# A gated mix of two long convolutions: a twisted length-2048 transform, a smaller set of kernel positions and no turn through DRAM

## The chip, the cores and the metric

The kernel runs on one core of a Trainium2 chip. The metric is the device time of one execution in microseconds (us). The engines are called PE (matrix multiply; its weight loads are shown apart as PEld), DVE (vector), ACT (scalar), POOL and SP; the last two mostly issue transfers here.

## The reference

Two branches act on 2048 positions of 448 channels, and a gate mixes them.

```
g = sigmoid((u * gate_w).sum(channels))                  # one number for each position
dt = exp(log_dt);  l = bf16(0 .. 2047)                   # positions rounded to bf16
K[d, l] = real(sum over 256 modes n of C[d,n] * exp(dt[d]*A[d,n]*l) * dt[d]*B[d,n])
a = causal_convolution(K, u) + u * Dskip                 # by a padded FFT of 4096
kv = (sum over t of 4 of k[l - t] * shift_k[d, t]) * v
b = u * (causal_convolution(ssm_k, kv) + kv * ssm_D)
out = g * a + (1 - g) * b
```

Because the positions are rounded to bf16, only 641 different values of l occur among the 2048: all up to 256, then every second, every fourth and every eighth.

## The kernel before

A position is split as 64a + b with a below 32 and b below 64, and a channel as a group g (4), a part h (2) and an index dd (56). The transform works on matrices of 128 rows.

**Setup** (`Weights`, `kgen_load`, `kgen_setup`, L23 to L411) builds the cosine matrices and the table of powers of the modes. Power level k+1 is the square of level k in float32, eleven levels by four DVE operations each (L408 to L411); each is written in bf16 to a DRAM scratch `ed` and read back block by block as `kg_E`.

**The SSM kernel K** is made by `KGen.block` in 14 blocks of 32 channels (64 modes to a partition). DVE multiplies up all powers by `cmul` (L427 to L434: one product over four planes into `kg_P`, one sum), a table `TQ` of 32 entries and a table `TP` of 8 by 8; ACT spreads factors (`kg_Ex`, L481). Then 128 matmuls of 32 weight columns and 64 moving columns give the block's K at all 2048 positions (L516), and ACT copies it into `xcK`.

**The convolutions** run in four halves (branch B halves 0 and 1, then branch A halves 0 and 1), each by `conv_half` as a generator of steps. `stage_c` and `stage2` transform the kernel (`K`), then the data (`X`), in 33 frequency classes; the skip term is added by a matmul with two rows of weights in each class (`ind`). `_pointwise` forms the complex product in six DVE operations of 3696 elements. `stage_a` goes back; `turn_write` and `turn_read` send its result through DRAM to turn rows into columns; `stage_b` finishes, and DVE forms the gated output into `tB`.

The order of work is written by hand: between steps of `conv_half` one kernel block is put, and inside one engine instructions go in the order that the scheduler lays down, the block's first. The next block's tables may be started while the matmuls of this one run, since `TQ` has two buffers; `TP` has one. The core lines of a product and of a block are:

```python
V.tensor_tensor(out=P4[:], in0=in0, in1=in1, op=ALU.mult)                                            # L433
self.last_dve = V.tensor_tensor(out=dst, in0=P4[:, :, :, 0, :], in1=P4[:, :, :, 1, :], op=ALU.add)   # L434
last_mm = nc.tensor.matmul(pt[...], lhsT=TQ[:, :, comp, m], rhs=TP[:, :, comp, m, :], ...)           # L516
dst = vd.rearrange("vc b (h ch) -> h b vc ch", h=2)                                                  # L292, the turn
run(gA0, 1); kg_blocks(1)                                                                            # L805
```

## Time and profile before

| | before |
|---|---|
| device time, median of 3 runs | 760.3 us (760.16 to 760.59) |
| span of the profiled execution | 759.5 us |
| instructions | 9670 |
| DVE busy | 562.7 us (74%) |
| ACT busy | 358.1 us (47%) |
| PE busy | 310.4 us (41%) |
| moved by DMA | 53.89 MB in 129130 packets |

Busy time is the union of an engine's instructions in the trace. The chain that ended last is followed back from the last instruction to what released it, and so on to the start. A granted clock of 1.0 is TensorE's upper level (2.4 GHz), 0.5 its lower one (1.2 GHz), and values between are mixtures over a stretch.

### The profile page before, as it was taken

What the parts mean: (1) busy time and instruction counts of PE and PEld (TensorE: products, weight loads), DVE (VectorE), ACT (ScalarE), POOL (GpSimd) and SP (SyncE); (2) the same over time, 40 slices, a digit from 0 to 9 for tenths busy, and PEclk for the clock granted to TensorE, in tenths of its full rate; (3) what the DMA queues carried; (4) which work ended last, traced back from release to release, by engine and by line L of the source; (5) the groups of instructions that cost most, each with busy time, mean ns of one, the idle gap of its engine ahead of it and who ended that gap; (6) DMA issues with size and microseconds to landing.
All of it is one profiled execution on the core that took longest, in us unless ns stands there. A gap on an engine that the chain in (4) does not pass through costs nothing.

```text
span 759.5 us, 9670 instructions
## 1 busy us (share of the span) xinstructions
PE 310.4 (41%) x3878; PEld 252.7 (33%) x3878; DVE 562.7 (74%) x892; ACT 358.1 (47%) x514; POOL 12.8 (2%) x53
## 2 busy tenths in 40 slices
PE   0000003000036964074289664354448827595502
PEld 0000002000033754074267553343436726464501
DVE  4279999796698569989989599999892987325603
ACT  0425309846427392363365946334675635155200
POOL 0000000000100000000000000000000000000000
PEclk9999998555557688586595986556657777697655
DMA  1450900783811010409901104947100004600094
GB/s 43 86 102 21 227 5 0 166 225 97 173 42 42 3 42 1 90 2 174 200 1 44 42 1 101 176 99 127 14 0 2 2 0 70 125 2 1 11 183 97
DMA packets 129130, 53.89 MB, mean 71 GB/s; under 512 B 97213, under 2 KB 127293, under 8 KB 129085
## 3 DMA queue, kind: packets, MB, share of 16 engines
q1 hardware_dynamic: 65486, 22.17, 15.0%
q10 hardware_dynamic: 61582, 20.10, 14.0%
q0 software_dynamic: 2016, 11.01, 4.4%
q8 instruction: 30, 0.49, 0.3%
q14 instruction: 16, 0.12, 0.1%
HBM read 31.71 MB, written 20.19 MB: 68 GB/s over the span
## 4 chain that ended last, share of the span: by engine, by line
DVE 46%; PE 22%; ACT 15%; DMA 8%; issue 5%; ACTq 1%; DVEq 0%; SPq 0%; POOL 0%; POOLq 0%
DVE kg_P L433 15%; PE ps_s L211 10%; PE ps_kg L516 7%; DVE kg_TP L434 6%; ACT zs L585 4%; PE ps_a L211 3%; DVE kg_TQ L434 3%; DMA tq<-vd_A 2%; ACT kg_TP L499 2%; ACT kg_Ex L481 2%; DMA vd_A<-vs 2%; ACT X L667 2%; ACT xcU L789 1%; PE ps_b L211 1%; DVE kg_er L411 1%
## 5 line engine op out<-in xcount | busy, mean ns | idle before, releaser
L516 PE MATMUL ps_kg<-kg_TP,kg_TQ 128*32 128x64 bf16 x1792 | 95.8, 235 | 182.8 <-DVE kg_TP L434 182.8
L516 PEld LDWEIGHTS <-kg_TQ 128*32 128x32 bf16 x1792 | 95.0, 150 | 185.4 <-issue 184.7
L433 DVE TENSOR_TENSOR kg_P<-kg_TP,kg_Ex 128x2048 bf16<-128x2048 bf16 x98 | 120.1, 1225 | 48.0 <-ACT kg_TP L499 43.5
L481 ACT COPY kg_Ex<-kg_E 128x2048 bf16<-128x2048 bf16 x42 | 80.5, 1918 | 65.1 <-DVE kg_P L433 59.8
L211 PE MATMUL ps_s<-zs,s_C 128*128 128x112 bf16 x512 | 81.3, 237 | 27.0 <-ACT K L667 14.7
L434 DVE TENSOR_TENSOR kg_TP<-kg_P 128x1024 bf16<-128x1024 bf16 x98 | 67.8, 692 | 4.0
L433 DVE TENSOR_TENSOR kg_P<-kg_TQ,kg_E 128x2048 bf16<-128x2048 bf16 (+2 forms) x70 | 67.1, 958 | 3.1
L211 PE MATMUL ps_s<-zs,s_NS 128*128 128x112 bf16 x264 | 61.8, 239 | 0.0
L211 PE MATMUL ps_s<-zs,s_S 128*128 128x112 bf16 x248 | 58.5, 240 | 0.0
L211 PEld LDWEIGHTS <-s_C 128*128 128x128 bf16 x512 | 51.6, 108 | 11.2 <-DVE zs L591 1.2
L667 ACT CAST K<-ps_s 128x448 bf16<-128x448 f32 (+1 forms) x68 | 34.7, 522 | 41.3 <-PE ps_s L211 41.2
L211 PE MATMUL ps_a<-X,sa_C 128*128 128x112 bf16 x256 | 38.3, 234 | 38.1 <-DVE X L544 30.1
L163 PE MATMUL ps_tr<-sa_ident,s_C 128*128 128x128 bf16 x33 | 3.7, 313 | 115.8 <-DVE sa_ident L154 115.8
L585 ACT CAST xcK<-ps_kg 128x512 bf16<-128x512 f32 x14 | 8.2, 585 | 87.0 <-PE ps_kg L516 87.0
L585 ACT CAST zs<-ps_c 128x512 bf16<-128x512 f32 x84 | 44.1, 646 | 2.9 <-PE ps_c L211 2.8
L163 PEld LDWEIGHTS <-s_C 128*128 128x128 bf16 x33 | 3.4, 149 | 115.8 <-DVE sa_ident L154 115.8
L434 DVE TENSOR_TENSOR kg_TQ<-kg_P 128x1024 bf16<-128x1024 bf16 (+2 forms) x70 | 39.0, 557 | 2.1
L499 ACT COPY kg_TP<-kg_pin 128x1024 bf16<-128x1024 bf16 x14 | 27.6, 1970 | 25.0 <-DVE kg_pin L434 25.0
L211 PE MATMUL ps_b<-tq,WB 128*128 128x224 bf16 x128 | 23.4, 347 | 38.6 <-DMA tq<-vd_A 26.6
L211 PEld LDWEIGHTS <-s_S 128*128 128x128 bf16 x248 | 28.2, 114 | 18.0 <-issue 17.9
L591 DVE CAST zs<-ps_c 128x512 bf16<-128x512 f32 x14 | 9.6, 691 | 31.3 <-PE ps_c L211 17.4
L667 ACT CAST X<-ps_s 128x448 bf16<-128x448 f32 (+1 forms) x68 | 30.5, 594 | 3.4 <-PE ps_s L211 3.3
(211 smaller groups left out, 722.9 us busy)
## 6 DMA issues: line engine op xcount, KB each, us to landing
...
```

The source lines that it names most:

```text
L163: nc.tensor.transpose(out=pt[:, i, :], in_=src[:, k0 + i, :], identity=ident[:])
L211: ins = nc.tensor.matmul(*args, **kwargs)
L411: V.tensor_tensor(out=er[:], in0=t1[:], in1=t2[:], op=ALU.subtract)
L433: V.tensor_tensor(out=P4[:], in0=in0, in1=in1, op=ALU.mult)
L434: self.last_dve = V.tensor_tensor(out=dst, in0=P4[:, :, :, 0, :], in1=P4[:, :, :, 1, :], op=ALU.add)
L481: nc.scalar.copy(Ex[:], Et[:, 3 + jj].unsqueeze(3).to_broadcast([P, 4, MB, 8]))
L499: nc.scalar.copy(TP[:, 0], pin[:].rearrange("p e c m -> p c m e"))
L516: last_mm = nc.tensor.matmul(pt[dg * 32:(dg + 1) * 32, ddl, h, :].rearrange("p (eh el) -> p eh el", eh=8), lhsT=TQ[:, :, comp, m], rhs=TP[ ...
L585: nc.scalar.copy(dst, src)
L591: V.tensor_copy(dst, src)
L667: nc.scalar.copy(dst[:, :, k:k + n, :].rearrange("p r k c -> p k r c") if n == 2 else dst[:, :, k, :], pt2[:] if n == 2 else pt2[:, 0])
L789: nc.scalar.copy(xu_v[:, q4 * 14:(q4 + 1) * 14], un_v[:, q4 * 14:(q4 + 1) * 14])
```

## The change

The kernel is written anew around the same split of a position.

- **Transform.** 32 classes instead of 33, at odd multiples (a twist), so that no class is special. `fft` does stage c in 7 groups of four columns (28 matmuls of 256 moving columns) and stage 2 in 8 groups of four classes (128 matmuls of 112 moving columns); ACT copies 1024 and 896 elements at a time. The skip term is added to the kernel's first entry before the transform, so the two-row matmuls are gone. Stage c now writes its result `zs` with single bf16 elements 56 bytes apart, and takes its weights with a stride of 112 bytes.
- **Product and inverse.** `products` has three DVE operations (7168, 3584 and 3584 elements); sums are left to the accumulation of `inverse`. That takes the products as weights (stride 56 bytes) against a moving matrix of 256 columns, 112 matmuls to a half, so that its result already stands with the right rows and needs no turn through DRAM. A last stage of 128 matmuls of 56 moving columns reads it with strides of 256 and 512 bytes.
- **SSM kernel.** 8 blocks of 56 channels (112 modes to a partition). Powers are built for 21 entries of a Q table and 16 of a P table; 16 more of P come from one product that mirrors them with a table of magnitudes. A block has 224 matmuls of 32 weight columns and 32 moving columns (stride 448 bytes), and four successive ones go to four different column groups of the array. Their 641 positions (32 by 32 values held) are spread to 2048 by `gather`, 56 matmuls with selection matrices, once for each half of branch A.
- **Setup.** Cosines and powers come straight from ACT's sine and exponent of phases in integers, in place of squarings; power levels are no longer copied four times. The modes are turned by PE and not by transposing transfers. The gate's sum over channels is 112 matmuls instead of a DVE sum.
- **Buffers and queues.** All large tiles share one pool `big` of five buffers of 15,008 bytes. The table `kg_T` of a block has one buffer, as have `S` (with room for four blocks) and a tag `kx` that two gathered kernels and branch B's raw kernel share. The reads of `ed` go on SP's queue and not on POOL's; nearly all of SP's transfers are in one line with them.

The old classes and functions are taken out whole, so the core of the diff below shows what stands in their place; lines of `products` without a mark are common to both:

```diff
--- before.py
+++ after.py
...
+NV = 56
+NW = 28
+CW = 7
+NBLK = NV // CW
+M = 16 * CW
+NMODE = 896
+Q_LEVELS = (1, 2, 4, 256, 512)
+P_LEVELS = (8, 16, 32, 64)
+R_LEVELS = (8, 16, 32, 64, 128)
+LEVELS = P_LEVELS + Q_LEVELS
+NLEV = len(LEVELS)
...
+NQ = 21
+RS = NQ
+PS = NQ + 8
+NTQP = PS + 32
+E_P0 = 2 * NLEV
...
+def fft(nc, psum, pool, W, C2, cols, dst, evac):
+    C, S, N = C2
+    zs = pool.tile([P, 2, 32, 4, NW], bf16, name="zs", tag="big")
+    zw = zs[:].rearrange("p r k g w -> p w (r k g)")
+    for j in range(NW // 4):
+        pt = psum.tile([P, 4, 256], f32, name="ps_c", tag="ps")
+        for i in range(4):
+            nc.tensor.matmul(pt[:, i, :], lhsT=cols(4 * j + i), rhs=W[:], start=True, stop=True)
+        evac(zw[:, 4 * j:4 * j + 4, :], pt[:])
+    for kk in range(8):
+        pt = psum.tile([P, 2, 512], f32, name="ps_2", tag="ps")
+        for i in range(4):
+            k = 4 * kk + i
+            o = i * 112
+            zr = zs[:, 0, k].rearrange("p g w -> p (g w)")
+            zi = zs[:, 1, k].rearrange("p g w -> p (g w)")
+            re, im = pt[:, 0, o:o + 112], pt[:, 1, o:o + 112]
+            c, s, n = (t[:, k].rearrange("p h s -> p (h s)") for t in (C, S, N))
+            nc.tensor.matmul(re, lhsT=c, rhs=zr, start=True, stop=False)
+            nc.tensor.matmul(re, lhsT=s, rhs=zi, start=False, stop=True)
+            nc.tensor.matmul(im, lhsT=n, rhs=zr, start=True, stop=False)
+            nc.tensor.matmul(im, lhsT=c, rhs=zi, start=False, stop=True)
+        evac(dst[:, :, 4 * kk:4 * kk + 4, :].rearrange("p r k c -> p r (k c)"), pt[:, :, 0:448])
...
+def inverse(nc, psum, pool, R, G, T, X, evac, consume):
+    R1, R2, R3 = (r[:].rearrange("p h c -> p (h c)") for r in R)
+    U = pool.tile([P, NW, 2, 2, 64], bf16, name="U", tag="big")
+    prods = ((T[:, 0], R1), (T[:, 1], R2), (X[:, 0], R3), (X[:, 1], R3))
+    for j in range(NW // 4):
+        pt = psum.tile([P, 4, 256], f32, name="ps_a", tag="ps")
+        for i in range(4):
+            w = 4 * j + i
+            for n, (t, r) in enumerate(prods):
+                lhsT = t.rearrange("p k (g w) -> p (k g) w", w=NW)[:, :, w]
+                nc.tensor.matmul(pt[:, i, :], lhsT=lhsT, rhs=r, start=(n == 0), stop=(n == 3))
+        evac(U[:, 4 * j:4 * j + 4].rearrange("p w h r b -> p w (h r b)"), pt[:])
+    for b0 in range(0, 64, 16):
+        pt = psum.tile([P, 2, 512], f32, name="ps_b", tag="ps")
+        for i in range(16):
+            b = b0 + i
+            o = pt[:, i // 8, (i % 8) * 56:(i % 8) * 56 + 56].rearrange("p (h w) -> p h w", h=2)
+            for r in range(2):
+                nc.tensor.matmul(o, lhsT=G[:, b, r].rearrange("p g a -> p (g a)"),
+                                 rhs=U[:, :, :, r, b].rearrange("p w h -> p h w"), start=(r == 0), stop=(r == 1))
+        consume(b0, pt)
...
+def products(nc, pool, X, K):
     V = nc.vector
+    T = pool.tile([P, 2, 32, 112], bf16, name="T", tag="big")
+    fl = lambda ap: ap.rearrange("p k c -> p (k c)")
+    V.tensor_tensor(out=T[:].rearrange("p r k c -> p (r k c)"), in0=X[:].rearrange("p r k c -> p (r k c)"),
+                    in1=K[:].rearrange("p r k c -> p (r k c)"), op=ALU.mult)
+    V.tensor_tensor(out=fl(X[:, 0]), in0=fl(X[:, 0]), in1=fl(K[:, 1]), op=ALU.mult)
+    V.tensor_tensor(out=fl(X[:, 1]), in0=fl(X[:, 1]), in1=fl(K[:, 0]), op=ALU.mult)
+    return T
...
+        T = self.pool.tile([P, NTQP, 2, M], bf16, name="kg_T", tag="kg_T")
+        nc.scalar.copy(T[:, PS], Et[:, E_P0:E_P0 + 2])
+        nc.scalar.copy(T[:, 0], Et[:, E_Q0:E_Q0 + 2])
+        R = T[:, RS:RS + 8].rearrange("p n c m -> p (n c) m")
+        def level(dst, srcs, e, n):
+            P4 = self.pool.tile([P, 2, 4, 2, M], bf16, name="kg_P4", tag="kg_P4", bufs=2)
+            E = Et[:, 2 * LI[e]:2 * LI[e] + 2]
+            m = n // len(srcs)
+            for i, (lo, st) in enumerate(srcs):
+                if st == 1:
+                    V.tensor_tensor(out=P4[:, :, i * m:(i + 1) * m].rearrange("p v n c m -> p v (n c) m"),
+                                    in0=T[:, lo:lo + m].rearrange("p n c m -> p (n c) m").unsqueeze(1).to_broadcast([P, 2, 2 * m, M]),
+                                    in1=E.unsqueeze(2).to_broadcast([P, 2, 2 * m, M]), op=ALU.mult)
+                else:
+                    for v in range(2):
+                        V.tensor_tensor(out=P4[:, v, i * m:(i + 1) * m], in0=T[:, lo:lo + (m - 1) * st + 1:st],
+                                        in1=E[:, v].unsqueeze(1).unsqueeze(1).to_broadcast([P, m, 2, M]), op=ALU.mult)
+            V.tensor_tensor(out=T[:, dst:dst + n, 0], in0=P4[:, 0, 0:n, 0], in1=P4[:, 1, 0:n, 1], op=ALU.subtract)
+            V.tensor_tensor(out=T[:, dst:dst + n, 1], in0=P4[:, 1, 0:n, 0], in1=P4[:, 0, 0:n, 1], op=ALU.add)
+        def rlevel(n, e):
+            mg = Et[:, E_MAG + R_LEVELS.index(e)]
+            if n == 1:
+                V.tensor_tensor(out=R[:, 1], in0=Et[:, E_MAG], in1=mg, op=ALU.mult)
+            else:
+                V.tensor_tensor(out=R[:, n:2 * n], in0=R[:, 0:n], in1=mg.unsqueeze(1).to_broadcast([P, n, M]), op=ALU.mult)
+        nc.scalar.copy(R[:, 0], Et[:, E_MAG])
+        level(1, [(0, 1)], 4, 1)
+        level(PS + 1, [(PS, 1)], 8, 1)
+        rlevel(1, 16)
+        level(2, [(0, 1)], 2, 2)
+        level(PS + 2, [(PS, 1)], 16, 2)
+        rlevel(2, 32)
+        level(8, [(0, 1)], 256, 4)
+        level(PS + 4, [(PS, 1)], 32, 4)
+        rlevel(4, 64)
+        level(12, [(0, 1), (8, 1)], 512, 4)
+        level(PS + 8, [(PS, 1)], 64, 4)
+        rlevel(8, 128)
+        level(16, [(12, 2)], 512, 2)
+        level(PS + 12, [(PS + 4, 1)], 64, 4)
+        level(18, [(16, 1)], 512, 2)
+        level(4, [(0, 1)], 1, 4)
+        lo = T[:, PS:PS + 16]
+        ap = [list(x) for x in lo.ap]
+        back = bass.AP(lo.tensor, lo.offset + 15 * 2 * M, [ap[0], [-2 * M, 16], [M, 2], [1, M]])
+        V.tensor_tensor(out=T[:, PS + 16:PS + 32], in0=back, in1=R.unsqueeze(2).to_broadcast([P, 16, 2, M]), op=ALU.mult)
+        level(20, [(18, 1)], 512, 1)
...
+        pt = self.psum.tile([P, 2 * CW, 32], f32, name="ps_k", tag="psk")
+        for hw in range(2 * CW):
+            h, w = divmod(hw, CW)
+            for hf in range(2):
+                for c in range(2):
+                    for g in range(4):
+                        m = ((hf * 4 + g) * 2 + h) * CW + w
+                        r0 = T[:, PS, c, m:m + 1]
+                        rhs = bass.AP(r0.tensor, r0.offset, [list(r0.ap[0]), [32 * M + (1 - 2 * c) * M, 2], [2 * M, 16]])
+                        nc.tensor.matmul(pt[32 * g:32 * g + 32, hw, :].rearrange("p (i j) -> p i j", i=2),
+                                         lhsT=T[:, 0:32, c, m], rhs=rhs, start=(hf == 0 and c == 0), stop=(hf == 1 and c == 1),
+                                         tile_position=(0, 32 * g))
+        evac(S[:].rearrange("p b (h v) -> p h v b", h=2)[:, :, v0:v0 + CW, :], pt[:].rearrange("p (h w) b -> p h w b", h=2))
...
+    def unit(e_re, e_im, off, out=None):
+        ph = tmp.tile([P, 2, NMODE], i32, name="ks_ph", tag="t8", bufs=2)
+        V.tensor_scalar(out=ph[:, 0], in0=f[:], scalar1=e_re * turn, scalar2=QUARTER + off, op0=ALU.mult, op1=ALU.add)
+        V.tensor_scalar(out=ph[:, 1], in0=f[:], scalar1=e_im * turn, scalar2=off, op0=ALU.mult, op1=ALU.add)
+        cs = tmp.tile([P, 2, NMODE], bf16, name="ks_cs", tag="t4", bufs=4)
+        s = nc.scalar.activation(cs[:].rearrange("p c m -> p (c m)"), low16(ph[:].rearrange("p c m -> p (c m)")), ACT.Sin, scale=PHASE)
+        after(tc, s, last["exp"])
+        last["sin"] = s
+        return cs
...
+    for e in LEVELS:
+        if e == Q_LEVELS[0]:
+            magnitudes(Q_LEVELS)
+        cs = unit(e, e if e in P_LEVELS else -e, 0.0)
+        E = tmp.tile([P, NBLK, 2, M], bf16, name="ks_E", tag="t4", bufs=4)
+        V.tensor_tensor(out=E[:].rearrange("p b c m -> p c b m"), in0=cs[:].rearrange("p c (b m) -> p c b m", b=NBLK),
+                        in1=bm(magof[e]).unsqueeze(1).to_broadcast([P, 2, NBLK, M]), op=ALU.mult)
+        store(E, 2 * LI[e])
...
+    big = ctx.enter_context(tc.tile_pool(name="big", bufs=NBIG))
+    kx = ctx.enter_context(tc.tile_pool(name="kx", bufs=1))
+    psum = ctx.enter_context(tc.tile_pool(name="psum", bufs=3, space=PSUM))
+    psk = ctx.enter_context(tc.tile_pool(name="psk", bufs=2, space=PSUM))
...
+        kv = bigt([P, 64, 112], "kv")
+        for b0 in (0, 32):
+            for i, tau in enumerate((3, 2, 1, 0)):
+                src = kt[:, b0 + 3 - tau:b0 + 35 - tau, :]
+                wb = wt[:, tau, :].unsqueeze(1).to_broadcast([P, 32, 112])
+                dst = kv[:, b0:b0 + 32, :]
+                if i == 0:
+                    V.tensor_tensor(out=dst, in0=src, in1=wb, op=ALU.mult)
+                else:
+                    t = bigt([P, 32, 112], "kvt")
+                    V.tensor_tensor(out=t[:], in0=src, in1=wb, op=ALU.mult)
+                    V.tensor_tensor(out=dst, in0=dst, in1=t[:], op=ALU.add)
+            V.tensor_tensor(out=dst, in0=dst, in1=vt[:, b0:b0 + 32, :], op=ALU.mult)
...
+        pg = psk.tile([P, 64], f32, name="ps_gate", tag="psk")
+        for l in range(112):
+            nc.tensor.matmul(pg[:], lhsT=ones[:], rhs=ug[:, :, l], start=(l == 0), stop=(l == 111))
+        gt = wp.tile([P, 64], f32, name="gt")
+        sg = nc.scalar.activation(gt[:], pg[:], ACT.Sigmoid)
+        og = wp.tile([P, 64], bf16, name="og")
+        V.tensor_scalar(out=og[:], in0=gt[:], scalar1=-1.0, scalar2=1.0, op0=ALU.mult, op1=ALU.add)
+        V.tensor_tensor(out=ug[:], in0=uu[:], in1=og[:].unsqueeze(2).to_broadcast([P, 64, 112]), op=ALU.mult)
...
+    kgp = ctx.enter_context(tc.tile_pool(name="kgp", bufs=1))
+    kge = ctx.enter_context(tc.tile_pool(name="kge", bufs=2))
+    kg = KGen(tc, kgp, kge, psk, ed, nc.sync)
+    S = kx.tile([P, 32, 56], bf16, name="S")
...
+    def epilogue_B(H):
+        def consume(b0, pt):
+            for i in range(2):
+                o = ug[:, b0 + 8 * i:b0 + 8 * i + 8, :].rearrange("p b (h v) -> p b h v", h=2)[:, :, :, H * NW:(H + 1) * NW]
+                V.tensor_tensor(out=o, in0=pt[:, i, 0:448].rearrange("p (b h w) -> p b h w", b=8, h=2), in1=o, op=ALU.mult)
+        return consume
...
+    blocks(1)
+    XB = forward(kv, 0)
+    blocks(1)
+    T = products(nc, big, XB, KB0)
+    inverse(nc, psum, big, R, G, T, XB, evac, epilogue_B(0))
+    blocks(1)
+    KB1 = spectrum_B(1)
+    blocks(1)
+    KT = kernel_A()
+    XB = forward(kv, 1)
+    blocks(1)
+    T = products(nc, big, XB, KB1)
+    inverse(nc, psum, big, R, G, T, XB, evac, epilogue_B(1))
+    blocks(1)
...
+    def spectrum_A(KT, H):
+        k0 = KT[:, 0, :].rearrange("p (h v) -> p h v", h=2)
+        V.tensor_tensor(out=k0, in0=k0, in1=dA[:].rearrange("p (h v) -> p h v", h=2)[:, :, H * NW:(H + 1) * NW], op=ALU.add)
+        K = bigt([P, 2, 32, 112], "K")
+        cols = KT[:].rearrange("p b (h w) -> p w (b h)", h=2)
+        fft(nc, psum, big, WcK, C2, lambda w: cols[:, w], K, evac)
+        return K
...
+    KA = spectrum_A(KT, 0)
+    blocks(1)
+    XA = forward(uu, 0)
+    T = products(nc, big, XA, KA)
+    blocks(1)
+    inverse(nc, psum, big, R, G, T, XA, evac, epilogue_A(0))
+    XA = forward(uu, 1)
+    KT = kernel_A()
+    KA = spectrum_A(KT, 1)
+    T = products(nc, big, XA, KA)
+    inverse(nc, psum, big, R, G, T, XA, evac, epilogue_A(1))
```

## Rows read from the trace of the kernel before

**Rows 1.** Page, part 1: busy us of each engine, its share of the span, instructions.

```profile
PE 310.4 (41%) x3878; PEld 252.7 (33%) x3878; DVE 562.7 (74%) x892; ACT 358.1 (47%) x514; POOL 12.8 (2%) x53
```

**Rows 2.** Windows of three stretches: length, busy us by engine, granted clock, DMA share, GB/s.

```profile
0.00:204.00 204.00, 6.36 (x66) 5.62 (x66) 154.03 (x341) 90.51 (x92) 4.18 (x18) 0.81 0.46 106
204.00:550.00 346.00, 189.54 (x2480) 156.23 (x2481) 300.51 (x403) 181.47 (x263) 8.42 (x33) 0.69 0.32 66
550.00:760.00 210.00, 114.53 (x1332) 90.82 (x1331) 108.15 (x149) 86.14 (x160) 0.23 (x2) 0.70 0.24 45
```

**Rows 3.** Page, part 4: the chain that ended last, by engine and by line.

```profile
DVE 46%; PE 22%; ACT 15%; DMA 8%; issue 5%; ACTq 1%; DVEq 0%; SPq 0%; POOL 0%; POOLq 0%
DVE kg_P L433 15%; PE ps_s L211 10%; PE ps_kg L516 7%; DVE kg_TP L434 6%; ACT zs L585 4%; PE ps_a L211 3%; DVE kg_TQ L434 3%; DMA tq<-vd_A 2%; ACT kg_TP L499 2%; ACT kg_Ex L481 2%; DMA vd_A<-vs 2%; ACT X L667 2%; ACT xcU L789 1%; PE ps_b L211 1%; DVE kg_er L411 1%
```

**Rows 4.** That chain near the end: start us, us, what.

```profile
719.05 12.17 DMA vd_A<-vs
731.97 8.84 DMA tq<-vd_A
```

**Rows 5.** Groups by line and shape, DVE: count, then busy us, mean ns of one.

```profile
L433 DVE TENSOR_TENSOR kg_P<-kg_TP,kg_Ex 128x2048 bf16<-128x2048 bf16 x98 | 120.1, 1225 | 48.0 <-ACT kg_TP L499 43.5
L434 DVE TENSOR_TENSOR kg_TP<-kg_P 128x1024 bf16<-128x1024 bf16 x98 | 67.8, 692 | 4.0
L434 DVE TENSOR_TENSOR kg_pin<-kg_P 128x128 bf16<-128x128 bf16 x14 | 3.2, 226 | 0.5
L742 DVE TENSOR_TENSOR ksacc<-ksacc,vt 128x3584 bf16<-128x3584 bf16 x2 | 4.0, 2018 | 0.0
L702 DVE TENSOR_TENSOR gprod<-un,gw 128x7168 bf16<-128x7168 bf16 x1 | 3.9, 3882 | 0.0
L762 DVE SCALAR_TENSOR_TENSOR tB<-ps_b,omg,un_e 128x224 bf16<-128x224 f32 x32 | 12.3, 444 | 2.8 <-PE ps_b L211 2.7
```

**Rows 6.** Timeline, DVE, independent small operations: start us, us.

```profile
2.18 0.15 DVE L52 TENSOR_SCALAR wc_a<-wc_a 128x1 f32<-128x1 f32 x1
2.24 0.15 DVE L51 TENSOR_SCALAR wb_vc<-w_pidx_f 128x1 f32<-128x1 f32 x1
```

**Rows 7.** Line L382, DVE with one float32 input: ns min/median/max.

```profile
L382 DVE TENSOR_SCALAR kg_th<-kg_th x1: 621/621/621, 51.4 to 51.4; 128x896 f32<-128x896 f32 x1
```

**Rows 8.** Groups by line and shape, ACT copies.

```profile
L585 ACT CAST xcK<-ps_kg 128x512 bf16<-128x512 f32 x14 | 8.2, 585 | 87.0 <-PE ps_kg L516 87.0
L481 ACT COPY kg_Ex<-kg_E 128x2048 bf16<-128x2048 bf16 x42 | 80.5, 1918 | 65.1 <-DVE kg_P L433 59.8 <-issue 5.2
L589 ACT CAST zs<-ps_c 128x512 bf16<-128x512 f32 x14 | 7.8, 594 | 3.5 <-PE ps_c L211 3.4
L499 ACT COPY kg_TP<-kg_pin 128x1024 bf16<-128x1024 bf16 x14 | 27.6, 1970 | 25.0 <-DVE kg_pin L434 25.0
```

**Rows 9.** Windows of the kernel blocks' matmuls alone: length, PE, ACT, granted clock.

```profile
220.50:227.40 6.90, 6.83 (x128) 0.00 (x0) 0.59 0.01 2
600.30:607.10 6.80, 6.80 (x128) 0.00 (x0) 1.00 0.02 5
```

**Rows 10.** Windows of dense transform matmuls, columns as in Rows 2.

```profile
666.80:680.30 13.50, 13.50 (x151) 9.02 (x149) 1.04 (x3) 7.45 (x14) 0.00 (x0) 1.00 0.00 1
708.20:714.20 6.00, 5.93 (x64) 5.93 (x64) 2.76 (x8) 2.64 (x8) 0.00 (x0) 0.50 0.00 0
```

**Rows 11.** Timeline, PE, inside the first of these windows: start us, us.

```profile
667.90 0.21 PE L211 MATMUL ps_s<-zs,s_C 128*128 128x112 bf16 x1
667.95 0.21 PE L211 MATMUL ps_s<-zs,s_S 128*128 128x112 bf16 x1
668.10 0.22 PE L211 MATMUL ps_s<-dA,ind 2*128 2x112 bf16 x1
668.25 0.22 PE L211 MATMUL ps_s<-zs,s_C 128*128 128x112 bf16 x1
```

**Rows 12.** Group of the kernel blocks' matmuls: count, then busy us, mean ns.

```profile
L516 PE MATMUL ps_kg<-kg_TP,kg_TQ 128*32 128x64 bf16 x1792 | 95.8, 235 | 182.8 <-DVE kg_TP L434 182.8
```

More of the change, by code (lines that the diff above doesn't have):

```diff
@@ L14 @@
 i32 = mybir.dt.int32
+i16 = mybir.dt.int16
 PSUM = bass.MemoryType.PSUM
 DRAM = bass.MemoryType.DRAM
[L17 to L18 removed]
 P = 128
[L20 to L204 removed]
@@ L414 @@
[L414 to L436 removed]
+PHASE = 6.2831845 / 65536
@@ new lines, with after @@
+QUARTER = 16384.0
+HALF = 32768.0
+NV = 56
[9 more added lines that the diff above has]
+NLEV = len(LEVELS)
+LI = {e: i for i, e in enumerate(LEVELS)}
+NQ = 21
[3 more added lines that the diff above has]
+E_P0 = 2 * NLEV
+E_Q0 = E_P0 + 2
+E_MAG = E_Q0 + 2
+ENT = E_MAG + len(R_LEVELS)
+NBIG = 5
+def after(tc, ins, before):
+    tc.add_manual_dep(ins.ins, before.ins.name,
+                      mybir.DependencyInfo(mybir.DependencyClass.NoSync, mybir.DependencyReason.DATA),
+                      reason="order on one engine")
@@ L585, in evac_act, with evac @@
+    def evac(dst, src):
         nc.scalar.copy(dst, src)
[L587 to L609 removed]
```

1020 lines of the change are left out of this document (344 added, 676 removed).

## The prediction

> **What bounds the kernel now.** I read the windows first, because three stretches have different limits [rows 2]. Up to 204 us there is setup: DVE is busy 154 of 204 us and PE has almost nothing. From 204 to 550 us DVE is busy 300.5 of 346 us: it is the bound, and what it does there is mostly the power tables of the kernel blocks. From 550 us on no engine is full (DVE 108, PE 115, ACT 86 of 210 us): steps wait for each other. The sums of busy time [rows 1] hide this. The chain of waits agrees: 46% of it is DVE, with the block lines L433 and L434 in front, and 8% is DMA [rows 3]. Near the end two of its longest pieces are the turn through DRAM, 12.17 us out and 8.84 us back [rows 4].
>
> **Prices.** A bf16 product of two tensors on DVE takes 692 ns for 1024 elements and 1225 ns for 2048 [rows 5]: 0.52 ns an element and 160 ns fixed, and the rows of 128, 3584 and 7168 elements (226, 2018, 3882 ns) lie on that line. Independent neighbours overlap: two operations of 150 ns start 60 ns apart [rows 6]. One float32 input without a second tensor costs 621 ns for 896 elements [rows 7]. ACT copies 512 elements in 585 ns and 2048 in 1918 ns, so 1024 cost about 1.03 us and 896 about 0.92 us [rows 8]. Dense PE work of 112 columns takes 93 ns a matmul at the lower clock (64 in 5.93 us) [rows 10] and 50 ns at the upper one, while each two-row skip matmul has 150 ns on either side of it [rows 11]. A block's 128 matmuls take 6.8 us, 53 ns each, at either clock [rows 9].
>
> **Setup, 204 us now.** I list DVE's new work from the diff. Cosine matrices and small tables: 16 to 24 us. Mode tables: 20 phase operations at 0.62, nine products of 1792 elements at 1.09, about 14 more: 37 us, in place of the squarings. The shifted keys: 16 operations of 3584 elements as before, 32 us. Gate products: 3.9 us, and 3.9 to 7.6 us for the second, whose repeated factor stands in the innermost direction; I take 7.6. Small rest: 5 us. The sum is 105 to 112 us. DVE was busy 0.755 of the old setup [rows 2]; with that share setup takes 140 to 148 us. Its waits change rather than go: the transposing loads and squarings leave, but the temporary tiles of the keys need a slot of the five-slot pool that the first kernel spectrum holds, and the gate waits for a load of u into a slot that the keys free. The block tiles follow in the memory of the setup's temporaries. I take **142 us**; at DVE's sum with no idle time it would be 108, at a busy share of 0.65 170.
>
> **A kernel block.** The levels have 35 new entries at 6 x 112 elements, the R table 15 x 112 and the mirror 32 x 112: 28,784 elements at 0.52 are 15.0 us. Its 46 operations cost 0.16 us fixed where one waits for the other, some 0.07 where not: about 6 us with the small gaps. So **21 us** (19 to 24), against seven pairs of 1.225 and 0.692 us and smaller ones, some 23 us, before; but 8 blocks and not 14: 168 us for about 320.
>
> Its 224 matmuls at 53 ns are **11.9 us**. Half the columns to a matmul should give half the time, yet 53 ns at both clocks shows that columns were not what set it, so I keep 53. The lower bound is 27 ns (columns halve it), 6 us; the upper one is in the rivals. The single `kg_T` now shows: the next block's ACT copies into it, and behind them all its levels on DVE, wait until PE has read the last column. That wait, 11.9 us and 1.5 us for the copies, is open to products and epilogues only. So a block's period is 34.5 us, and eight are 276 us.
>
> **A transform.** Stage c: 7 ACT copies of 1.03 us and a start, 7.9 us. Its writes land singly, 56 bytes apart. Writing in runs of four elements costs nothing visible (594 against 585 ns), while *reading* with a large stride doubles ACT's copy (1970 ns for 1024) [rows 8]. A strided single write is in no row; it lies between 1.03 and 1.97 us, and I take 1.03 as the written row is the nearest. Stage 2: 128 matmuls, 6.4 us at 50 ns, 11.9 us at 93; with a clock between the levels (0.69 and 0.70 in the last two windows [rows 2]) 8.5, and 1.3 for the last copy. A transform is **17.7 us**; seven stand behind the setup.
>
> **Product and inverse.** Products: 14,336 elements in three operations, 7.9 us, against six of 3696 elements, 12.5 us by the same price. Stage a: 112 matmuls of 256 columns, 12.8 us by the upper price per column, 23.8 by the lower; its weights are strided, so 19, and 1.3 to copy. Last stage: 128 small matmuls, 6.4 to 11.9 us, taken 9, and 1.7 for DVE to finish. An inverse is **31 us**. The turn, 21 us on the last one [rows 4], has no successor; nor have the skip matmuls, some 0.2 us in each of 33 classes [rows 11].
>
> **Gather.** 20,608 columns in 56 matmuls: 8.6 us at the upper price and 17 at the lower if they go one by one, a quarter if the column groups work together. I take 9.
>
> **The sum.** On DVE's chain behind setup: eight periods, 276 us; products and epilogues of the first three inverses, 43 us (an epilogue operation reads 448 PSUM elements; 224 take 444 ns [rows 5], and at twice 0.52 ns for each more that is 0.68 us), of which half fits into the waits for `kg_T`, so 21; then what follows the last block: copy 0.6, gather 9, transform 17.7, products 7.9, inverse 31, store about 8, together 74. That is **371 us**. PE's own chain is nearly as long: transforms 124, products between 32, inverses 124, block matmuls 96, gathers 18 and the store 8 are 402, less some 40 of the block matmuls that fit where PE waits for ACT or products: 362. Two chains of one length on in-order queues cost each other time. In the old DVE-bound stretch 13% of DVE's time was lost to waits [rows 2]; the largest of these is already priced, so I add half of it, **25 us**. The profiled execution: 142 + 371 + 25 = 538 us; the median stood 0.8 us above its span of 759.5 us, so the time is **539 us**. Below that I cannot separate a few us of transfers: SP now issues level stores, raw kernels, block tables and u in one line, and a raw kernel that waits for a slot holds the table loads behind it.
>
> **A rule on strides.** The row shows 1970 ns where contiguous data would cost 1030 [rows 8]. The Trainium skill, SBUF — State Buffer, section Specifications, says that SBUF lines have 16 bytes and that accesses that go to a new line each time pay a penalty; the trace agrees for that read. By it the new strides would make this kernel about 604 us, against 539 without it.
>
> **Rivals.**
> 1. *Every single-element stride doubles.* For: the strided ACT read [rows 8], and block matmuls that do not gain from the upper clock [rows 9]. Against: short runs written by ACT are free. ACT's stage c costs 0.94 us more in each of 49 copies, 46 us, and stage a goes from 19 to 23.8 us four times, 19 us: 539 + 65 = **604 us**.
> 2. *Column groups work side by side*, so that a block's matmuls take a quarter, 3 us. For: four successive ones use different groups. Against: nothing shows two together. Eight times 9 us leave both chains; DVE's is then 299 us, and PE's, which loses half of its hidden 40 us with them, 402 - 72 - 20 = 310 and decides: 142 + 310 + 25 and the 0.8 make **478 us**. The Trainium skill, TensorEngine Tiling (Array Packing), section Tiling Modes, says that tiles execute independently; no run here shows it.
> 3. *Blocks and transforms hardly overlap*, since five slots and single buffers make each wait for the other. Behind setup PE's 402 us and the blocks' 168 us on DVE then stand in a row: 142 + 402 + 168 = **712 us**; half of that loss gives 640.
> 4. *Slower than before: changing the column group empties the array.* Place: each of 1792 block matmuls. For: a matmul of another form costs 150 ns on either side [rows 11]; one that drains takes its whole 235 ns [rows 12]. At these prices 1792 x (97 to 182) ns are added: **713 to 865 us**. Slower from 177 ns a matmul. Against: the old blocks change groups every 32 matmuls and stay at 53 ns [rows 9].
>
> **How the numbers follow.** The forecast has 0.45, with its own range 500 to 575 us (setup 130 to 155, losses 10 to 45). Rival 1 has 0.23, rival 2 0.13, rival 3 0.13, rival 4 0.06. From 465 to 645 us the range holds all but rival 4, the far half of rival 3 and the lower tail of rival 2, about 0.17. A measurement of this kernel tells 0.2% from no change. Half of rival 4 is slower, and a little of a worse rival 3: slower 0.04, same 0.01, faster 0.95.
>
> **What would show it.** Right: the first block's product starts near 142 us; block products sum to about 168 us on DVE and recur every 34 us; block matmuls stay at 53 ns; no transfers of `vd`; stage c copies near 1.03 us; after the last block some 75 us. Wrong: copies of 1024 elements near 2 us; block matmuls at 150 ns or at 13; DVE idle much above 13 us in a period; a setup past 170 us; a spectrum that stands still for a slot of `big`.

## The result and the profile after

The changed kernel takes 693.59 us (median of four runs, 690.9 to 694.58) where the kernel before took 760.23 us beside it. The ratio is 0.9135 with a 95% interval of 0.9102 to 0.9167: faster by 8.6%. The forecast was 539 us and its range ended at 645 us. So the direction was right, and the gain was under a third of the one forecast. The profiled execution took 694.0 us, with a span of 692.2 us.

The page of the changed kernel first, parts 1 and 4: busy us and share of each engine, then the chain that ended last by engine and by line.

```profile
PE 285.0 (41%) x4272; PEld 253.0 (37%) x4272; DVE 302.7 (44%) x554; ACT 413.0 (60%) x238; POOL 10.6 (2%) x122
...
ACT 42%; PE 27%; DVE 21%; issue 4%; ACTq 2%; POOL 1%; DMA 1%; POOLq 0%; SPq 0%
ACT zs L508 32%; PE ps_a L240 7%; PE ps_b L248 7%; DVE kg_P L294 5%; PE ps_k L342 4%; PE ps_gate L602 2%; DVE kv L590 2%; DVE T L257 2%; DVE kg_T L301 2%; DVE kg_T L302 2%; PE ps L223 1%; ACT X L508 1%; DVE kvt L589 1%; PE ps L225 1%; PE ps L224 1%
```

DVE did give up what was forecast: 562.7 us busy before [rows 1], 302.7 now, and 46% of the chain before [rows 3], 21% now. But a new engine leads: ACT, busy 413 us, and one of its lines is a third of the chain. All ACT copies go through the helper in L508, so the line has to be taken apart by tile. The next view groups by line and shape (busy us, mean ns of one, idle before and its releaser):

```profile
L508 ACT CAST zs<-ps_c 128x1024 bf16<-128x1024 f32 x56 | 248.0, 4831 | 53.6 <-PE ps_c L212 53.6
...
L342 PE MATMUL ps_k<-kg_T 128*32 128x32 bf16 x1792 | 31.1, 241 | 21.3 <-DVE kg_T L301 12.1 <-issue 9.1
...
L508 ACT CAST U<-ps_a 128x1024 bf16<-128x1024 f32 x28 | 28.5, 1025 | 35.9 <-PE ps_a L240 35.8
...
L508 ACT CAST S<-ps_k 128x448 bf16<-128x448 f32 x8 | 18.2, 2275 | 103.0 <-PE ps_k L342 103.0
```

The rows of `zs` and `U` are the whole case in small. Both read 1024 float32 elements from PSUM and write 1024 bf16 elements, on one engine. `U` is written densely and takes 1025 ns, which is the price that the forecast gave to any such copy. `zs` is written as single elements 56 bytes apart and takes 4831 ns. `S` is written as singles 112 bytes apart: 448 elements take 2275 ns. The row of L342 holds the block matmuls, which come up below.

The windows, with the stretches of [rows 2] (the last one now ends with the span), show where the time stands:

```profile
0.00:204.00 204.00, 49.89 (x472) 43.80 (x472) 110.95 (x157) 126.68 (x74) 10.61 (x122) 0.82 0.42 78
204.00:550.00 346.00, 160.20 (x3063) 144.22 (x3064) 169.98 (x370) 199.45 (x119) 0.00 (x0) 0.65 0.11 23
550.00:692.00 142.00, 74.95 (x740) 64.96 (x737) 21.76 (x28) 86.88 (x47) 0.00 (x0) 0.62 0.07 14
```

DVE, which had been the bound from 204 to 550 us, is now busy in half of that stretch. The chain near the end says what holds it up (start us, us, what):

```profile
608.30 18.78 ACT zs L508 x5
627.15 2.66 issue
629.81 9.17 ACT zs L508 x2
...
643.34 4.96 ACT K L508 x6
648.32 3.90 DVE T L257
652.25 2.03 DVE X L259
654.28 1.95 DVE X L260
656.27 13.17 PE ps_a L240 x103
...
670.53 12.66 PE ps_b L248 x128
```

Seven `zs` copies take some 30 us of a transform for which 17.7 us were forecast in all. The list of waits (us in total, times, longest) names the same tile for PE:

```profile
PE ps_c L212 <- ACT zs L508: 110.8, 32, 5.5
...
DVE kg_P L294 <- ACT kg_T L285: 98.2, 8, 33.0
...
PE ps L223 <- ACT zs L508: 84.2, 8, 12.0
```

Stage c cannot go on because its PSUM tile is not yet copied, and stage 2 cannot begin before the last copy: 195 us of waits at two lines. The middle row is DVE's: a kernel block begins with small ACT copies into `kg_T`, and these stand in ACT's queue among the `zs` copies. The chain shows it at one block, where the first small copy is followed by seven `zs` copies before the next one runs:

```profile
484.67 0.70 ACT kg_T L284
485.37 30.59 ACT zs L508 x7
```

### The profile page after: what moved, and what is told of

Same layout as the page of the kernel before. It is cut to its first block, busy times and chain, and to the rows that moved or that the text cites. A ratio compares the mean times of both kernels' runs of the same rounds, so it can differ in the third digit from the quotient of the medians.

```text
span 692.2 us, 9722 instructions
## 1 busy us (share of the span) xinstructions
PE 285.0 (41%) x4272; PEld 253.0 (37%) x4272; DVE 302.7 (44%) x554; ACT 413.0 (60%) x238; POOL 10.6 (2%) x122
## 4 chain that ended last, share of the span: by engine, by line
ACT 42%; PE 27%; DVE 21%; issue 4%; ACTq 2%; POOL 1%; DMA 1%; POOLq 0%; SPq 0%
ACT zs L508 32%; PE ps_a L240 7%; PE ps_b L248 7%; DVE kg_P L294 5%; PE ps_k L342 4%; PE ps_gate L602 2%; DVE kv L590 2%; DVE T L257 2%; DVE kg_T L301 2%; DVE kg_T L302 2%; PE ps L223 1%; ACT X L508 1%; DVE kvt L589 1%; PE ps L225 1%; PE ps L224 1%
## 5 line engine op out<-in xcount | busy, mean ns | idle before, releaser
L508 ACT CAST zs<-ps_c 128x1024 bf16<-128x1024 f32 x56 | 248.0, 4831 | 53.6 <-PE ps_c L212 53.6
L294 DVE TENSOR_TENSOR kg_P<-kg_T,kg_E 128x896 bf16<-128x896 bf16 (+2 forms) x104 | 73.5, 745 | 98.2 <-ACT kg_T L285 98.2
L223 PE MATMUL ps<-zs,s_C 128*128 128x112 bf16 x256 | 61.7, 249 | 84.2 <-ACT zs L508 84.2
L508 ACT CAST S<-ps_k 128x448 bf16<-128x448 f32 x8 | 18.2, 2275 | 103.0 <-PE ps_k L342 103.0
L240 PE MATMUL ps_a<-sa_r,T 128*128 128x256 bf16 x224 | 46.3, 293 | 44.2 <-DVE T L257 30.7
L224 PE MATMUL ps<-zs,s_S 128*128 128x112 bf16 x256 | 61.8, 250 | 0.0
L225 PE MATMUL ps<-zs,s_N 128*128 128x112 bf16 x256 | 61.6, 249 | 0.0
L226 PE MATMUL ps<-zs,s_C 128*128 128x112 bf16 x256 | 61.4, 249 | 0.0
L248 PE MATMUL ps_b<-U,sb_G 128*128 128x56 bf16 x512 | 50.8, 275 | 3.9 <-ACT U L508 3.9
L248 PEld LDWEIGHTS <-sb_G 128*128 128x128 bf16 x512 | 49.9, 122 | 4.8 <-issue 4.8
L508 ACT CAST U<-ps_a 128x1024 bf16<-128x1024 f32 x28 | 28.5, 1025 | 35.9 <-PE ps_a L240 35.8
L212 PE MATMUL ps_c<-Wc,sk 128*128 128x256 bf16 x56 | 12.7, 385 | 89.6 <-DVE sk L566 59.6
L240 PE MATMUL ps_a<-sa_r,X 128*128 128x256 bf16 x224 | 45.3, 288 | 3.4 <-DVE X L260 2.1
L342 PE MATMUL ps_k<-kg_T 128*32 128x32 bf16 x1792 | 31.1, 241 | 21.3 <-DVE kg_T L301 12.1
L342 PEld LDWEIGHTS <-kg_T 128*32 128x32 bf16 x1792 | 29.0, 148 | 23.9 <-DVE kg_T L301 12.3
L212 PE MATMUL ps_c<-Wc,kv 128*128 128x256 bf16 x56 | 12.7, 381 | 59.7 <-DVE kv L591 32.2
L307 DVE TENSOR_TENSOR kg_T<-kg_E 128x112 bf16<-128x112 bf16 x8 | 1.7, 217 | 76.1 <-PE ps_k L342 71.5
L508 ACT CAST X<-ps 128x896 bf16<-128x896 f32 x32 | 27.8, 930 | 11.0 <-PE ps L226 7.9
## 6 DMA issues: line engine op xcount, KB each, us to landing
kt<-in_B_k_dram ACTq DMA_DIRECT2D x2, 448.0 KB, 12.8
```

The lines of the kernel that those rows point to most:

```text
L212: nc.tensor.matmul(pt[:, i, :], lhsT=cols(4 * j + i), rhs=W[:], start=True, stop=True)
L223: nc.tensor.matmul(re, lhsT=c, rhs=zr, start=True, stop=False)
L224: nc.tensor.matmul(re, lhsT=s, rhs=zi, start=False, stop=True)
L225: nc.tensor.matmul(im, lhsT=n, rhs=zr, start=True, stop=False)
L226: nc.tensor.matmul(im, lhsT=c, rhs=zi, start=False, stop=True)
L240: nc.tensor.matmul(pt[:, i, :], lhsT=lhsT, rhs=r, start=(n == 0), stop=(n == 3))
```

## The experiments

Theory: the price of a scattered write is the step that failed, and the rest of the sum holds. Rivals: ACT itself is slow on such a copy and another engine would not be; a price for each run of elements, whatever its length; and a rest of the sum that is wrong as well, so that the copies hide a second bound. Ratios are to the kernel before, run beside each kernel.

**Runs of four.** The same bytes go to the same places; only the order in which ACT walks through them changes, so that four neighbours are written one after the other:

```diff
-        evac(zw[:, 4 * j:4 * j + 4, :], pt[:])
+        evac(zw[:, 4 * j:4 * j + 4, :].rearrange("p i n -> p n i"), pt[:].rearrange("p i n -> p n i"))
```

> Only the order in which ACT walks a stage c copy changes: the same 1024 elements to the same places, but four neighbours (8 bytes) one after the other, read from PSUM with a step of 1 KB. Theory A (the price is that of single 2-byte writes 56 bytes apart): the copy falls from 4.83 to about 1.1 to 1.3 us, 56 copies give back some 200 us on ACT, and the kernel takes 470 to 530 us. Rival B (the price comes from the PSUM side, or from any copy of this size out of two banks): the copy stays at 4.5 us or more and the time near 693 us. Rival C (ACT is slow here but not on the path): the copy falls and the time stays above 650 us.

Measured: 514.65 us (513.76 to 515.52), ratio 0.6776 (0.675 to 0.6801). The time falls by 179 us with one line. By shape and by the chain, of this kernel:

```profile
L508 ACT CAST zs<-ps_c 128x1024 bf16<-128x1024 f32 x56 | 53.0, 1054 | 54.3 <-PE ps_c L212 54.3
```

```profile
DVE 34%; PE 33%; ACT 17%; DMA 5%; SPq 5%; issue 5%; ACTq 0%; DVEq 0%
```

A copy costs 1054 ns, 3.78 us less; 56 of them are 212 us, and 179 of those were on the path. What is left comes near the picture that the forecast drew: DVE and PE have like shares of the chain. DVE's wait for `kg_T` in the list above falls from 98.2 to 32.6 us.

**Runs of two.** The walk is changed so that two neighbours, four bytes, are written together:

```diff
+        zj = zw[:, 4 * j:4 * j + 4, :].rearrange("p (a b) n -> p a n b", b=2)
+        pj = pt[:].rearrange("p (a b) n -> p a n b", b=2)
-        evac(zw[:, 4 * j:4 * j + 4, :], pt[:])
+        evac(zj, pj)
```

> As runs4, with two neighbours (4 bytes) at a time, so twice as many separate runs. Theory A, with a price for each run that is written: half of the single-element price above the fixed part, about 2.3 to 2.5 us a copy and 550 to 590 us in all. Theory A', a price only for 2-byte writes that fill no 4-byte word: about 1.1 us and the same time as runs4. Rival B: 4.5 us or more and 693 us.

Measured: 516.97 us in a single run. By shape:

```profile
L510 ACT CAST zs<-ps_c 128x1024 bf16<-128x1024 f32 x56 | 54.9, 1096 | 54.1 <-PE ps_c L212 54.0
```

A copy takes 1096 ns: two elements are nearly as good as four. A price for each run would have left half of the excess, 1.9 us a copy; in this copy, writing four bytes at a time removes it.

**The same copy on DVE.** The scattered write stays and moves to the other engine, which has time to spare:

```diff
-        evac(zw[:, 4 * j:4 * j + 4, :], pt[:])
+        nc.vector.tensor_copy(zw[:, 4 * j:4 * j + 4, :], pt[:])
```

> The stage c copies go to DVE with the access pattern of the changed kernel. If the price belongs to ACT's writes: a copy takes about 1.25 us on DVE (1.04 ns an element and a fixed part), DVE gains 70 us of work, ACT loses 271, and the kernel takes 480 to 540 us. If scattered single writes cost every engine alike: 4 to 5 us a copy on DVE, and the time stays between 640 and 720 us.

Measured: 693.32 us (692.6 to 695.53), ratio 0.9138 (0.9107 to 0.9169), no different from the changed kernel. By shape:

```profile
L213 DVE CAST zs<-ps_c 128x1024 bf16<-128x1024 f32 x56 | 249.1, 4706 | 10.1 <-PE ps_c L212 10.1
...
L223 PE MATMUL ps<-zs,s_C 128*128 128x112 bf16 x256 | 59.5, 242 | 91.3 <-DVE zs L213 91.3
```

4706 against 4831 ns: ACT is not what is slow. The price goes with the writing, and stage 2's wait follows the copy to its new engine.

**The stride moved to the reader.** `zs` is laid out as `[P, NW, 2, 32, 4]`, so that ACT writes densely and stage 2 on PE reads its moving columns as single elements 512 bytes apart:

```diff
-    zs = pool.tile([P, 2, 32, 4, NW], bf16, name="zs", tag="big")
+    zs = pool.tile([P, NW, 2, 32, 4], bf16, name="zs", tag="big")
...
-            zr = zs[:, 0, k].rearrange("p g w -> p (g w)")
+            zr = zs[:, :, 0, k, :].rearrange("p w g -> p g w")
```

> The buffer of stage c is laid out so that ACT writes 1024 elements in one piece, and the stride moves to the reader: stage 2 streams its 112 columns as single elements 512 bytes apart. Theory A: the copy takes 1.03 us. If PE streams strided columns at its usual rate, 47 to 93 ns a matmul and 470 to 530 us; if a strided column costs it double, 100 to 190 ns a matmul in stage 2, some 10 us more in each of eight transforms, and 540 to 600 us. Rival B: the copy stays at 4.5 us.

Measured: 625.36 us (624.47 to 627.3), ratio 0.8242 (0.8214 to 0.827). The copies are cheap (1044 ns), yet 111 us of the gain of the first experiment are gone, and the time is above the 540 to 600 us that were expected. A window inside stage 2 of this kernel, columns as in [rows 2]:

```profile
560.00:570.00 10.00, 10.00 (x55) 6.46 (x53) 0.00 (x0) 2.94 (x4) 0.00 (x0) 0.50 0.00 0
```

The timeline inside it (start us, us):

```profile
560.06 0.37 PE L224 MATMUL ps<-zs,s_S 128*128 128x112 bf16 x1
560.25 0.37 PE L225 MATMUL ps<-zs,s_N 128*128 128x112 bf16 x1
```

The window also counts matmuls that only reach into it; the starts stand 0.19 us apart. So a matmul of 112 columns takes 190 ns, where dense columns cost 93 ns at that clock [rows 10]. A moving operand of scattered elements costs PE some 1.7 ns a column.

**Prices measured by themselves.** The kernel with runs of four gets 16 more copies at its end, of the same 224 bf16 elements, into tiles that nothing reads; only the step and length of the writes differ (a name gives element and step in bytes; `two` is a pair of neighbours, `word` a float32):

```diff
+        v = v[:, 0:n * step].rearrange("p (n s) -> p n s", s=step)[:, :, 0:run]
+        copy(v, src.rearrange("p (n r) -> p n r", r=run))
...
+        price(copy, eng + "_half_by_eight", 4, 1, bf16)
+        price(copy, eng + "_two_by_sixtyfour", 32, 2, bf16)
+        price(copy, eng + "_word_by_sixtyfour", 16, 1, f32)
```

> The kernel of runs4 with 16 extra copies of 224 bf16 elements behind the last result, eight on ACT and eight on DVE, out of one dense row of SBUF into scratch with different steps; the output is the same and the time some 8 us more. Theory A' (only writes that fill no 4-byte word and land in another line each time are dear): dense, two by 64 bytes and a 4-byte word by 64 bytes take about 0.4 us, single halves by 16, 32 and 64 bytes about 1.2 us (4.5 ns an element), halves by 4 bytes near the dense price, as the raw kernel's copy had 1.12 ns an element. If stride alone counts, words by 64 bytes cost as much as halves by 64. ACT and DVE alike.

Measured, by shape (the second number after the bar is ns of the one copy):

```profile
L709 ACT COPY act_half_by_sixtyfour<-ug 128x224 bf16<-128x224 bf16 x1 | 1.4, 1437 | 0.0
L709 ACT COPY act_half_by_thirtytwo<-ug 128x224 bf16<-128x224 bf16 x1 | 1.4, 1425 | 0.0
L709 ACT COPY act_half_by_sixteen<-ug 128x224 bf16<-128x224 bf16 x1 | 1.2, 1239 | 0.0
L709 DVE COPY dve_half_by_sixtyfour<-ug 128x224 bf16<-128x224 bf16 x1 | 0.9, 861 | 0.0
...
L709 ACT COPY act_half_by_eight<-ug 128x224 bf16<-128x224 bf16 x1 | 0.7, 672 | 0.0
L709 ACT COPY act_two_by_sixtyfour<-ug 128x224 bf16<-128x224 bf16 x1 | 0.7, 670 | 0.0
L709 ACT CAST act_word_by_sixtyfour<-ug 128x224 f32<-128x224 bf16 x1 | 0.6, 570 | 0.0
...
L709 ACT COPY act_half_by_four<-ug 128x224 bf16<-128x224 bf16 x1 | 0.4, 435 | 0.0
...
L709 ACT COPY act_dense<-ug 128x224 bf16<-128x224 bf16 x1 | 0.4, 377 | 17.3 <-DMA out_dram<-ug 17.3
...
L709 DVE COPY dve_dense<-ug 128x224 bf16<-128x224 bf16 x1 | 0.2, 219 | 5.4 <-DMA out_dram<-ug 5.4
```

Above the dense copy, ACT pays for each single bf16 element 0.3 ns at a step of 4 bytes, 1.3 at 8, 3.8 at 16 and 4.7 at 32 and 64 bytes (1437 - 377 = 1060 ns for 224). A float32 word at 64 bytes pays 0.9 ns, a pair of bf16 2.6 ns for both. So in these rows it is neither the step alone nor the small element alone that is dear, but an element of two bytes written far from the last one. The theory is not the whole of it. Pairs and words were expected at about 0.4 us and took 0.67 and 0.57, and a pair cost only 0.14 ns in the copy from PSUM above (1096 against 1025 ns for 512 pairs); why it costs more here is open, as the copies differ in source, type and step. Single elements paid 3.7 ns there (4831 against 1025 ns for 1024). Nor is DVE like ACT: it pays 2.9 ns at 64 bytes here, and its copy from PSUM took 4.6 ns an element in all, with no dense one beside it. Each of these copies ran once.

**The spectrum's copy in runs of seven**, on top of the runs of four:

```diff
-        evac(S[:].rearrange("p b (h v) -> p h v b", h=2)[:, :, v0:v0 + CW, :], pt[:].rearrange("p (h w) b -> p h w b", h=2))
+        evac(S[:].rearrange("p b (h v) -> p h b v", h=2)[:, :, :, v0:v0 + CW], pt[:].rearrange("p (h w) b -> p h b w", h=2))
```

> As runs4, and ACT also walks the copy of a block's result in runs of seven neighbours (14 bytes) where it wrote single elements 112 bytes apart. The same theory: the copy falls from 2.23 to about 0.6 us, eight times 1.6 us; most of them are not waited for, so the time falls by 3 to 13 us to 502 to 512. If the price has another cause, the copy stays at 2.2 us and the time at 515.

Measured: 509.0 us (505.63 to 511.82), ratio 0.6716 (0.6676 to 0.6757); the copy falls from 2230 to 619 ns. Eight times 1.6 us are 13 us, and the median moved by 5.6; the intervals of this kernel and of the one it is built on overlap, so the gain is likely but not settled.

**One column group at a time.** On top of the runs of four, the loop over the four column groups becomes the outermost of a block's matmuls, so that successive ones use the same group:

```diff
-        for hw in range(2 * CW):
-            h, w = divmod(hw, CW)
-            for hf in range(2):
-                for c in range(2):
-                    for g in range(4):
+        for g in range(4):
+            for hw in range(2 * CW):
+                h, w = divmod(hw, CW)
+                for hf in range(2):
+                    for c in range(2):
```

> As runs4, but a block's 224 matmuls are ordered by column group: 56 to one group before the next, where four successive ones went to four groups. If the groups work side by side (17.5 ns a matmul in place of the 53 forecast), one group alone gives 55 to 70 ns, 12 to 16 us a block, some 9 to 12 us more in each of eight blocks of which part is on the path: 550 to 610 us. If 32 moving columns are simply cheap, 17.5 ns and 515 us stay.

Measured: 585.82 us (583.54 to 590.39), ratio 0.7723 (0.7678 to 0.7768), 71 us slower than with the groups in turn. One block in the chain of this kernel:

```profile
184.30 12.47 PE ps_k L342 x224
```

The 224 matmuls of this block take 12.5 us (12.4 in two others), 55 ns each; by their number, the forecast's 53 ns and 11.9 us are what a block costs with one group at a time. All eight blocks, by shape, here and with the groups in turn (the kernel with runs of four):

```profile
L342 PE MATMUL ps_k<-kg_T 128*32 128x32 bf16 x1792 | 99.9, 231 | 14.7 <-DVE kg_T L301 14.6
...
L342 PE MATMUL ps_k<-kg_T 128*32 128x32 bf16 x1792 | 31.4, 241 | 22.0 <-DVE kg_T L301 13.0 <-issue 8.8
```

The changed kernel, too, runs them in turns: here 222 matmuls in one window of it, nearly all of them a block's (length, PE busy, granted clock, DMA share, GB/s):

```profile
359.68:363.26 3.58, 3.58 (x222) 1.00 0.02 5
```

16 ns each. With runs of four, a block's 224 at a granted clock of 0.50 (its matmuls alone):

```profile
184.30:190.00 5.70, 3.96 (x224) 3.70 (x224) 0.50 0.03 6
```

That is 17.7 ns a matmul, and with one group at a time the block from 184.30 us on also had 0.50. At that clock 32 dense columns one after the other would take 27 ns (93 ns for 112 [rows 10]), so 17.7 ns cannot be one matmul at a time: the four groups work side by side. The Trainium skill, TensorEngine Tiling (Array Packing), section Tiling Modes, says that tiles run in parallel; these two runs agree, with a factor of 12.47 / 3.96 = 3.1 at the same clock and not of four. What sets the 55 ns of one group is open. They are 1.7 ns for each of 32 moving columns that stand 448 bytes apart, the price of the other scattered columns; and in this order four successive matmuls also add to the same PSUM columns. No run takes these apart.

**The inverse's last stage reads runs.** On top of the runs of four, `U` is laid out with 28 neighbours for each reader. ACT writes it in runs of four, PE reads its moving columns in runs of 28:

```diff
-    U = pool.tile([P, NW, 2, 2, 64], bf16, name="U", tag="big")
+    U = pool.tile([P, 64, 2, 2, NW], bf16, name="U", tag="big")
+    uw = U[:].rearrange("p b h r w -> p b (h r) w")
...
-        evac(U[:, 4 * j:4 * j + 4].rearrange("p w h r b -> p w (h r b)"), pt[:])
+        evac(uw[:, :, :, 4 * j:4 * j + 4], pt[:].rearrange("p i (q b) -> p b q i", q=4))
...
-                                 rhs=U[:, :, :, r, b].rearrange("p w h -> p h w"), start=(r == 0), stop=(r == 1))
+                                 rhs=U[:, b, :, r, :], start=(r == 0), stop=(r == 1))
```

> As runs4, and the buffer between stage a and the last stage is laid out so that the last stage streams its 56 columns as two dense runs of 28, and ACT writes runs of four neighbours. If the stride of the moving columns sets the 99 ns of a last-stage matmul (strided columns took 190 ns for 112 in w_major, 1.7 ns a column), it falls to about 50 ns: 6 us less in each of four inverses, 490 to 500 us. If the weight load or DVE's epilogue sets it, 99 ns and about 515 us stay.

Measured: 494.13 us (492.44 to 497.74), ratio 0.6514 (0.6476 to 0.6553), 20.5 us less than with the runs of four alone. In the chain of this kernel:

```profile
416.51 1.00 PE ps_b L249 x32
...
417.54 1.69 DVE ept L647 x3
```

32 small matmuls take 1.00 us, 31 ns each, at a granted clock of 1.00. The strided ones take 99 ns: 128 in 12.66 us at a mean clock of 0.56 in the changed kernel and of 0.61 with runs of four, and 96 in 9.55 us at 0.73 there. So the clock does not set their price. All four last stages, by shape:

```profile
L249 PE MATMUL ps_b<-U,sb_G 128*128 128x56 bf16 x512 | 14.9, 190 | 6.7 <-ACT U L509 3.9 <-DVE ug L640 2.8
```

They kept PE busy for 50.8 us with the strided layout. Behind the last stage now stands DVE's epilogue. `U` still costs 1035 ns to write.

**All three together:** runs of four, the spectrum's copy and the inverse's layout.

> Stage c's zs, the spectrum S and the inverse's U are all written in runs of at least four elements, and the last stage reads dense runs of 28; nothing else differs from the changed kernel. If scattered single writes and scattered moving operands were the whole excess, the gains that the three edits gave alone add up: the run with runs of four for zs alone took 514.65 us, S alone gave a further 5.6 us, U alone a further 20.5 us, so about 488 to 490 us. The rival theory, that removing one wait only uncovers the next (epilogues on DVE behind the last stage, DVE's block chain behind the spectrum's copy), gives 493 to 500 us, little below the 494.13 us of the run with U alone. Copies: zs 1.05, S 0.62, U 1.03 us; last-stage matmuls 31 ns.

Measured: 483.82 us (482.32 to 486.15), ratio 0.6382 (0.6358 to 0.6407), where 488 to 490 us were expected. The gains add up, and a little more: 30.8 us below the runs of four, where the two edits alone gave 26.1. This version beats both kernels, the kernel before by 36% and the changed one by 30%. Its page:

```profile
PE 230.8 (48%) x4272; PEld 206.6 (43%) x4272; DVE 301.8 (63%) x554; ACT 206.5 (43%) x238; POOL 10.6 (2%) x122
...
DVE 43%; PE 21%; ACT 17%; DMA 7%; SPq 7%; issue 4%; ACTq 0%; DVEq 0%
```

DVE is in front again, at 63%, with the blocks' products as the largest line of the chain.

**The gate's second product later.** On top of all three, one DVE product of the setup is issued after the first block:

```diff
-        V.tensor_tensor(out=ug[:], in0=uu[:], in1=og[:].unsqueeze(2).to_broadcast([P, 64, 112]), op=ALU.mult)
...
     blocks(1)
+    V.tensor_tensor(out=ug[:], in0=uu[:], in1=og[:].unsqueeze(2).to_broadcast([P, 64, 112]), op=ALU.mult)
     XB = forward(kv, 0)
```

> The same kernel with the second gate product (7.6 us on DVE, which needs the gate's 112 matmuls and the sigmoid) issued after the first kernel block instead of before it. If the setup ends 23 us later than forecast because DVE stands still for the 13.6 us of the gate's matmuls, the first block's product starts some 21 us earlier (about 144 us instead of 165) and the time falls by the stall, about 14 us (the product itself is still DVE's to do), to about 475 us. The rival: the first transform of the data, which needs PE and ACT and the product kv, is what follows and does not start earlier, so that DVE only waits later; then the gain is under 4 us.

Measured: 490.69 us (489.35 to 492.66), ratio 0.6468 (0.6441 to 0.6494): 7 us slower, which neither theory said. The expectation also misread the kernel it starts from: the first block there begins at 147 us, before the gate's product, and is only interrupted by it, so there were 8 us to move and not 21. The chain of this kernel at its fifth block:

```profile
277.10 0.12 ACT kg_T L285
...
277.37 1.02 ACT zs L509
278.39 0.87 ACT KT L509 x2
...
284.63 2.75 ACT zs L509 x3
287.38 0.28 ACT kg_T L286
```

The block begins with small copies on ACT into `kg_T`. The first (L285) runs at 277.10 us, when PE has read the last column, but ten microseconds of `zs` and `KT` copies stand between it and the second (L286) in ACT's queue. Without the edit the two run one behind the other, at 278.45 and 278.73 us. The mirror of the second block (L332) was 3 us earlier than without the edit, that of the fifth 8 us later. So here the earlier start was lost to another order on the queue; whether that order follows from the edit in a way one could foresee stays open.

## Why the prediction was wrong

**The step that failed** is the first term of the transform: "a strided single write is in no row; it lies between 1.03 and 1.97 us, and I take 1.03 as the written row is the nearest". It is 4.83 us. Both bounds were wrong, and for one reason: the lower row wrote runs (of eight elements, as two groups of four stand side by side in memory; the prediction says four) and the upper one *read* with a stride [rows 8], so neither wrote single elements. The upper bound was an upper bound of nothing. At 56 copies this is 212 us of ACT and 179 us of the time, more than the whole difference between 539 and 693.59.

**Stage by stage**, in the spans: the first block's product was forecast at 142 us; it came at 184.7, and with runs of four at 148.0. From there to the end of the last block's mirror the forecast has 276 + 21 + 25 = 322 us; measured 357, and 265 with runs of four. The rest was forecast at 74 us; measured 150, and 101. Without the copies' excess the sum is 514 against 538, and three errors cancel in part, so that its nearness is partly luck:

- *Block matmuls*, 11.9 us forecast, 3.6 to 4.0 measured: 8 us a block, 64 in all. Rival 2's mechanism is true, shown by the experiment on column groups. DVE's wait for PE to have read the single `kg_T` is 29.3 us over seven blocks with runs of four, 4.2 each; in the changed kernel, where PE itself waits for the `zs` copies, it is 71.5. With runs of four the blocks recur every 33.3 us (47.1 in the changed kernel). The forecast had 34.5, but with 11.9 us of that wait in it, so this agreement is luck. Rival 2's sum, 478 us, is not reached even with runs of four: behind the setup it has 335 us and 366 were measured, and no run shows which of its terms fell short.
- *The tail*, 74 us forecast, 101 measured with runs of four. I had one transform behind the last block. The trace shows 24 us of the inverse before it, then both transforms of the last half in a row, 33 us: PE's queue holds them in the order written.
- *Strided operands on PE.* Stage a's weights were to cost, at 19 us; its 112 matmuls take 12.3 us at a granted clock of 1.00 and 13.2 at 0.86, near the 12.8 of dense columns at the upper price. The last stage's moving columns were to be cheap, at 9 us; they take 12.7, and 4 us when they stand together.

**Right:** a block's products on DVE sum to some 171 us over eight blocks (168 forecast), the products of a half take 7.9 us as priced, no transfer of `vd` is left, and with runs of four the setup ends 6 us late. Two slips in the sums change little: 20,608 columns at the price used for stage a are 9.2 us and not 8.6, and half of the way from 539 to rival 3's 712 us is 626 and not 640.

**Rival 1** (every single-element stride doubles, 604 us) named the place and the sign, at a quarter of the price: 0.94 us a copy, where 3.8 were measured; the rest of its 65 us, strided weights, did not show. The rule set beside it (the Trainium skill, SBUF — State Buffer, section Specifications: lines of 16 bytes, a penalty for going to a new one each time) does not explain the size. By it a float32 word at every 64 bytes, a new line each, should be dear, and two bf16 elements in one line should be cheap; measured are 0.9 ns for the word and 1.3 ns for the half words at a step of 8 bytes. **Rival 3** (640 to 712 us) comes near the measured time by its number alone: one line's copies gave the time back, with buffers and slots as they were, so what it names is not the cause. **Rival 4** is refuted, as a change of the column group does not empty the array but gains.
